# A decode layer on one core: wq as one transfer, finer last loads, and one copy moved to ScalarE

## The chip, the cores and the metric

The kernel runs on one core of one Trainium2 chip. The metric is device time in microseconds. "Median" is over the fast runs of a kernel: on one core that means that none was over 1.5% above the fastest of its kernel. A span quoted from a profile is about 2 us shorter than the time of the same execution (293.0 of 294.94 us for the kernel before). Each measurement is set against runs of the kernel before from the same rounds on the same chip.

## The reference, cut to what matters

A pre-norm decode step for a batch of 2 tokens of width 640: attention with 32 heads of 192 over the last 2048 positions of a cache, then a gated FFN of width 1536. Everything is bf16.

```python
x = A_x                                             # 2 x 1 x 640
h = x + attention(layernorm(x), k_cache, v_cache, wq, wo)
h2 = h + (gelu(ln @ w_gate) * (ln @ w_up)) @ w_down # ln = layernorm(h)
# wq: 640 x 6144    wo: 6144 x 640    w_gate, w_up: 640 x 1536    w_down: 1536 x 640
# K and V used: 2 x 32 x 2048 x 192 each, i.e. 50.3 MB each
```

The core has to read 122.29 MB for two tokens of output. There is little arithmetic per byte, so loads are the natural limit.

## The kernel before

All loads go through one DMA queue, issued in order by SyncE (called SP in the profile), into a ring of six slots of 24 KB per partition. K and V come in 16 groups of 3 MB each. A load may be issued when everything it overwrites has been used. Its issue order is K 0, wq, K 1, V 0, K 2, V 1, K 3, V 2, ..., then wo's last parts, w_gate, w_up and w_down.

```python
WQC = ((0, 2), (2, 4), (4, 5))
WDC = ((0, 3), (3, 6), (6, 9), (9, 12))
...
K_AT = (0, SLOT, 2 * SLOT, 3 * SLOT)
V_AT = (4 * SLOT, 5 * SLOT)
WQ_AT = (2 * SLOT, 3 * SLOT, 5 * SLOT)
WO_AT = (3 * SLOT, 3 * SLOT, 2 * SLOT, 0)
WD_AT = (2 * SLOT + 15360, 2 * SLOT + 19200, 15360, 19200)
...
        def load_wq():
            wq = A_wq.rearrange("(p c) n -> p c n", c=NC5)
            for i, (c0, c1) in enumerate(WQC):
                load(("wq", i), WQ_AT[i], 2 * (c1 - c0) * HQ * DH, wq[:, c0:c1, :],
                     lambda v: v.rearrange("p (c n) -> p c n", n=HQ * DH), f"wq{i}")
...
        def load_ffn():
            for key, at, w in (("wg", K_AT[1], B_w_gate), ("wu", K_AT[3], B_w_up)):
                load(key, at, 2 * NC5 * F, w.rearrange("(p c) f -> p c f", c=NC5),
                     lambda v: v.rearrange("p (c f) -> p c f", c=NC5), key)
            wd = B_w_down.rearrange("(r p j) n -> r p j n", p=128, j=3)
            for i, (f0, f1) in enumerate(WDC):
                load(("wd", i), WD_AT[i], 2 * (f1 - f0) * D, wd[i],
                     lambda v: v.rearrange("p (s n) -> p s n", n=D), f"wd{i}")
```

The queries are 80 matmuls over wq's five chunks; each part is used as it lands:

```python
        def q_rows():
            for i, (c0, c1) in enumerate(WQC):
                wq, wtoks = where["wq", i]

                def fn(e, c0=c0, c1=c1, wq=wq):
                    for c in range(c0, c1):
                        for J in range(4):
                            for r in range(4):
                                ins = e.matmul(tps[0][32 * r:32 * (r + 1), 0:384], lhsT=xnT[:, c, 32 * J:32 * (J + 1)],
                                               rhs=wq[:, c - c0, 1536 * J + 384 * r:1536 * J + 384 * (r + 1)],
                                               start=(c == 0 and J == 0), stop=(c == NC5 - 1 and J == 3), tile_position=(0, 32 * r))
                    return ins

                pe(fn, R=["xnT"] + wtoks, X=[("t", 0)])
                done(("wq", i))
```

At the end, when the loads run out, the FFN is a chain of small steps: normalised h (`hnT`), 20 matmuls with w_gate, a copy, transposes, gelu; then 20 matmuls with w_up, a copy, transposes, the product `uT`; then 48 matmuls with w_down in the blocks of `WDC`, a copy to `yrow`, and the store.

```python
        def ffn_columns(bank, xt, i):
            dve(lambda e: e.tensor_copy(grow[0:98, :], bank[0:98, 0:384]), W=["grow"], X=[xt])

            def fn(e):
                for j in range(3):
                    ins = e.transpose(tps[i][:, 128 * j:128 * j + 98], grow[0:98, j:384:3], identf[0:98, 0:98])
                return ins

            pe(fn, R=["grow", "identf"], X=[("t", i)])
            return tps[i][:, 0:384].rearrange("p (j r y) -> p r j y", j=3, y=32)[:, :, :, 0:2]
...
        ffn_in(sps, "s", "wg")
        gT = ffn_columns(sps, "s", 0)
        pe(h_rows, R=["hrow", ("hsel", 0), ("hsel", 1)], X=["m1"])
        ...                                         # gelu on VectorE and ScalarE
        ffn_in(ops_, "o", "wu")
        vT = ffn_columns(ops_, "o", 1)
        dve(tt(uT[...], vT, rjb(ga[:, 0, :]), ALU.mult), R=["ga0"], W=["uT"], X=[("t", 1)])
        for i, (f0, f1) in enumerate(WDC):
            ...                                     # 4 matmuls for each of the rows f0..f1 of w_down
        dve(lambda e: e.tensor_copy(yrow[0:98, :], m1[0:98, 0:160]), W=["y"], X=["m1"])
```

## Time and profile before

| | before |
|---|---|
| time, median of 3 runs | 294.95 us (294.79 to 294.95) |
| profiled span | 293.0 us |
| read from memory | 122.29 MB |
| busy: PE, DVE, ACT | 68%, 44%, 33% |
| the loading queue's share of 16 DMA engines | 97.8% |

Five lines of the page of the kernel before. The first two cut the span into 40 slices of 7.3 us: the busy share of the 16 DMA engines in tenths, and what they moved. The third is the loading queue (packets, MB, share of 16 engines' span), the fourth the chain of waits followed back from the end, the fifth the costliest group: its line, engine and operands, then busy us and mean ns of one, then idle us before it and what ended the idling.

```profile
DMA  7999999999999999999999999999999999999993
GB/s 279 436 427 433 431 440 435 430 425 430 425 420 438 430 433 427 430 430 430 430 421 436 430 430 430 430 430 433 430 430 430 430 430 430 430 430 426 430 406 125
q1 hardware_dynamic: 6632, 122.29, 97.8%
DMA 72%; PE 23%; SPq 2%; DVE 2%; issue 1%; ACT 0%
L549 PE MATMUL tps<-identf,ring 128*128 128x128 f32 x768 | 116.5, 320 | 46.4 <-DMA ring<-in_A_k_cache_dram 45.5
```

The DMA engines are full from the second slice to the last but one, near 430 GB/s. The Trainium skill, "DMA: Bandwidth & Descriptors", section "Where 436 GB/s comes from", gives 435.2 GB/s as the ceiling; this trace agrees with that to about 1%. PE mostly waits for K. So, leaving aside an earlier start of the loads, which the change doesn't touch, two things can make this kernel shorter: fewer DMA nanoseconds, or less work after the last byte has landed.

The timeline of the kernel before, at the end (start us, duration us, engine, line, instruction, and in brackets the idle time before it and who ended it; DMA landings show as releasers). PEld is PE's weight load.

```profile
284.26 0.71 PE L797 MATMUL m<-hrow,hsel 98*2 98x160 f32 x8
284.93 0.10 PEld L778 LDWEIGHTS ops<-ring,hnT 128*2 128x2 bf16 x8 [0.56 <-DMA ring<-in_B_w_up_dram]
284.93 1.77 PE L778 MATMUL ops<-ring,hnT 128*2 128x384 bf16 x20
286.75 0.56 DVE L785 COPY grow<-ops 98x384 f32<-98x384 f32 x1 [0.53 <-PE ops L778]
288.16 0.18 DVE L402 TENSOR_TENSOR uT<-tps,ga 128x24 bf16<-128x24 f32 x1 [0.86 <-PE tps L789]
288.40 1.84 PE L824 MATMUL m<-ring,uT 128*2 128x160 bf16 x48 [0.28 <-DVE uT L402]
289.67 0.23 PEld L824 LDWEIGHTS m<-ring,uT 128*2 128x2 bf16 x12 [0.24 <-DMA ring<-in_B_w_down_dram]
290.29 0.32 DVE L830 CAST yrow<-m 98x160 bf16<-98x160 f32 x1 [1.94 <-PE m L824]
```

The last 12 of the 48 w_down matmuls wait for the last landing (289.62 us in the trace's landing records, which hold the completion of each load by each of the 16 DMA engines; a load has landed when the last of the 16 is in).

The start, on SyncE's own row of the timeline: after K 0, wq, K 1 and V 0 have been issued, SyncE waits until wq's parts have been used.

```profile
1.45 1.63 SPq L342 DMA_DIRECT2D ring<-in_A_wq_dram  x3
...
20.49 0.54 SPq L342 DMA_DIRECT2D ring<-in_A_k_cache_dram  x1
31.98 0.54 SPq L342 DMA_DIRECT2D ring<-in_A_v_cache_dram  x1
32.56 0.61 SPq L342 DMA_DIRECT2D ring<-in_A_k_cache_dram  x1
```

These are K 2, V 1 and K 3.

### The profile page before, as it was taken

What the parts mean: (1) busy time and instruction counts of PE and PEld (TensorE: products, weight loads), DVE (VectorE), ACT (ScalarE), POOL (GpSimd) and SP (SyncE); (2) the same over time, 40 slices, a digit from 0 to 9 for tenths busy, and PEclk for the clock granted to TensorE, in tenths of its full rate; (3) what the DMA queues carried; (4) which work ended last, traced back from release to release, by engine and by line L of the source; (5) the groups of instructions that cost most, each with busy time, mean ns of one, the idle gap of its engine ahead of it and who ended that gap; (6) DMA issues with size and microseconds to landing.
All of it is one profiled execution on the core that took longest, in us unless ns stands there. A gap on an engine that the chain in (4) does not pass through costs nothing.

```text
span 293.0 us, 5065 instructions
## 1 busy us (share of the span) xinstructions
PE 198.8 (68%) x2141; PEld 153.0 (52%) x2141; DVE 128.5 (44%) x311; ACT 95.7 (33%) x119; POOL 8.4 (3%) x35
## 2 busy tenths in 40 slices
PE   2573586858677298849493597659696869666764
PEld 1451264838474285628281575356666666533432
DVE  5950364433447045525264155415365435532332
ACT  2150144433442143616161144234343434520000
POOL 3000100000000000000000000000000000000000
PEclk9996569795979579998899599969797968997755
DMA  7999999999999999999999999999999999999993
GB/s 279 436 427 433 431 440 435 430 425 430 425 420 438 430 433 427 430 430 430 430 421 436 430 430 430 430 430 433 430 430 430 430 430 430 430 430 426 430 406 125
DMA packets 6654, 122.44 MB, mean 418 GB/s; under 512 B 754, under 2 KB 756, under 8 KB 1396
## 3 DMA queue, kind: packets, MB, share of 16 engines
q1 hardware_dynamic: 6632, 122.29, 97.8%
q8 instruction: 7, 0.11, 0.2%
q14 instruction: 3, 0.02, 0.0%
q10 hardware_dynamic: 12, 0.00, 0.0%
HBM read 122.29 MB, written 0.00 MB: 417 GB/s over the span
## 4 chain that ended last, share of the span: by engine, by line
DMA 72%; PE 23%; SPq 2%; DVE 2%; issue 1%; ACT 0%
DMA ring<-in_A_k_cache_dram 54%; PE tps L549 16%; DMA ring<-in_A_wq_dram 10%; DMA ring<-in_A_wo_dram 9%; SPq L342 2%; PE ops L652 1%; PE m L703 1%; PE m L824 1%; PE sps L778 1%; PE ops L778 1%; PE m L685 1%; PE tps L789 1%; PE tps L571 1%; PE m L722 0%; DVE grow L785 0%
## 5 line engine op out<-in xcount | busy, mean ns | idle before, releaser
L549 PE MATMUL tps<-identf,ring 128*128 128x128 f32 x768 | 116.5, 320 | 46.4 <-DMA ring<-in_A_k_cache_dram 45.5
L549 PEld LDWEIGHTS tps<-identf,ring 128*128 128x128 f32 x768 | 107.3, 168 | 49.8 <-DMA ring<-in_A_k_cache_dram 46.9
L558 ACT ACTIVATE ktr<-tps 128x1024 bf16<-128x1024 bf16 x80 | 79.4, 1023 | 87.4 <-PE tps L549 87.4
L561 DVE COPY ktr<-tps 128x1024 bf16<-128x1024 bf16 x112 | 74.0, 687 | 74.5 <-PE tps L549 73.8
L627 ACT ACTIVATE eexp<-sm,nm 128x512 bf16<-128x512 f32 x16 | 11.5, 721 | 64.5 <-DVE nm L625 64.5
L652 PE MATMUL ops<-ring,ering 128*32 128x384 bf16 x512 | 24.4, 334 | 4.7 <-DMA ring<-in_A_v_cache_dram 4.7
L608 PE MATMUL sps<-ktr,rq 128*16 128x512 bf16 x384 | 25.9, 404 | 1.1 <-POOL rq L402 1.1
L616 DVE CUSTOM_DVE_ANT_1 sm<-sps,mska 128x512 f32<-128x512 f32 x16 | 11.1, 691 | 34.9 <-PE sps L608 34.9
L652 PEld LDWEIGHTS ops<-ring,ering 128*32 128x32 bf16 x512 | 12.5, 97 | 13.0 <-DMA ring<-in_A_v_cache_dram 6.0
L608 PEld LDWEIGHTS sps<-ktr,rq 128*16 128x16 bf16 x384 | 9.4, 90 | 12.1 <-issue 2.1
L623 PEld LDWEIGHTS m<-mrhs,pm 128*128 128x128 bf16 x16 | 1.5, 96 | 22.8 <-DVE mrhs L398 22.8
L623 PE MATMUL m<-mrhs,pm 128*128 128x16 bf16 x16 | 2.9, 184 | 14.7 <-DVE mrhs L398 14.7
L402 POOL TENSOR_TENSOR rq<-qs,mask 128x96 bf16<-128x96 bf16 x16 | 5.6, 359 | 195.9 <-PE sps L608 164.9
L571 PE MATMUL tps<-ring,xnT 128*32 128x384 bf16 x80 | 5.7, 444 | 7.4 <-DMA ring<-in_A_wq_dram 7.3
L402 DVE TENSOR_TENSOR ering<-m,mask 128x256 bf16<-128x256 f32 x16 | 6.7, 418 | 3.6 <-PE m L636 3.6
L571 PEld LDWEIGHTS tps<-ring,xnT 128*32 128x32 bf16 x80 | 2.4, 120 | 10.3 <-DMA ring<-in_A_wq_dram 8.3
L454 ACT ACTIVATE lt<-m,eps_t 128x2 f32<-128x2 f32 x2 | 0.5, 262 | 20.1 <-PE m L452 20.1
L594 DVE CAST qs<-ops 128x384 bf16<-128x384 f32 x1 | 0.6, 558 | 14.4 <-PE ops L589 14.4
L636 PE MATMUL m<-sel,eexp 128*128 128x64 bf16 x64 | 5.3, 213 | 1.2 <-ACT eexp L627 1.2
L636 PEld LDWEIGHTS m<-sel,eexp 128*128 128x128 bf16 x64 | 4.9, 114 | 1.7 <-DVE nm L625 1.3
L703 PE MATMUL m<-ring,ot 128*2 128x320 bf16 x96 | 4.9, 338 | 1.1 <-DMA ring<-in_A_wo_dram 1.1
L402 DVE TENSOR_TENSOR orow<-m,wm 128x1536 bf16<-128x1536 f32 x3 | 5.3, 1750 | 0.0
(113 smaller groups left out, 84.2 us busy)
## 6 DMA issues: line engine op xcount, KB each, us to landing
ring<-in_A_k_cache_dram SPq DMA_DIRECT2D x16, 3072.0 KB, 32.7
ring<-in_A_v_cache_dram SPq DMA_DIRECT2D x16, 3072.0 KB, 27.6
ring<-in_A_wq_dram SPq DMA_DIRECT2D x2, 3072.0 KB, 21.0
ring<-in_A_wo_dram SPq DMA_DIRECT2D x3, 1920.0 KB, 19.4
ring<-in_B_w_gate_dram SPq DMA_DIRECT2D x1, 1920.0 KB, 30.9
ring<-in_B_w_up_dram SPq DMA_DIRECT2D x1, 1920.0 KB, 27.0
ring<-in_B_w_down_dram SPq DMA_DIRECT2D x4, 480.0 KB, 28.9
ring<-in_A_wq_dram SPq DMA_DIRECT2D x1, 1536.0 KB, 27.9
```

What stands on the lines that cost most here:

```text
L342: P.op("sp", lambda e, v=v, src=src: e.dma_start(v, src), W=toks + [("sem", sem)], dma=sem)
L402: return lambda e: e.tensor_tensor(out=out, in0=a, in1=b, op=op)
L549: ins = e.transpose(tps[bi][:, 128 * u:128 * (u + 1)], kv[:, off:off + 128], identf[:, :])
L558: act(lambda e, dst=dst, bv=bv: e.activation(out=dst, in_=bv, func=ACT.Copy), W=[("kt", n)], X=[("t", bi)])
L561: dve(lambda e, dst=dst, bv=bv: e.tensor_copy(dst, bv), W=[("kt", n)], X=[("t", bi)], cls=0)
L571: ins = e.matmul(tps[0][32 * r:32 * (r + 1), 0:384], lhsT=xnT[:, c, 32 * J:32 * (J + 1)], rhs=wq[:, c - c0, 1536 * J + 384 * r:1536 * J + ...
L608: ins = e.matmul(sps[32 * ch:32 * ch + 16, :], lhsT=rq[:, g % 4, k, :], rhs=ktr[:, k // 2, 1024 * ch + k % 2:1024 * (ch + 1):2], start=(k ...
L616: dve(lambda e: e.tensor_tensor_reduce(out=sm[:, :].rearrange("p (u x) -> p u x", u=4), in0=sps[:, :].rearrange("p (u x) -> p u x", u=4), ...
L627: act(lambda e: e.activation(out=eexp[:, :], in_=sm[:, :], func=ACT.Exp, bias=nm[:, 0:1], scale=1.0, accum_out=zr[:, g % 4:g % 4 + 1]), R= ...
L636: ins = e.matmul(o, lhsT=eexp[:, 128 * u:128 * (u + 1)], rhs=sel64[:, :], start=True, stop=True)
L652: ins = e.matmul(ops_[32 * r:32 * (r + 1), 0:384], lhsT=ering[:, g % 4, t, :], rhs=vv[:, 384 * t:384 * (t + 1)], start=(g % 4 == 0 and t < 4),
L703: ins = e.matmul(m1[32 * r:32 * r + 2, 192:512], lhsT=ot[:, kk, :], rhs=wo[:, kk - k0, 320 * h:320 * (h + 1)], start=(kk == 1 or J < 2 and ...
```

## The change

Its intent, read from the diff: fewer and longer rows for wq (60 KB per partition, contiguous in memory) by laying it over two and a half slots; less PE work behind each of the last landings, by loading w_up as 4 + 1 chunks and w_down's last block as 2 + 1 rows; and the copy of up out of PSUM on ScalarE, which is idle there. The diff, with the second half of the mechanical edits cut:

```diff
-WQC = ((0, 2), (2, 4), (4, 5))
-WDC = ((0, 3), (3, 6), (6, 9), (9, 12))
+WDC = ((0, 3), (3, 6), (6, 9), (9, 11), (11, 12))
+WUC = ((0, 4), (4, 5))
 BIG = 1.0e9
-K_AT = (0, SLOT, 2 * SLOT, 3 * SLOT)
-V_AT = (4 * SLOT, 5 * SLOT)
-WQ_AT = (2 * SLOT, 3 * SLOT, 5 * SLOT)
-WO_AT = (3 * SLOT, 3 * SLOT, 2 * SLOT, 0)
-WD_AT = (2 * SLOT + 15360, 2 * SLOT + 19200, 15360, 19200)
+K_AT = (0, SLOT, 3 * SLOT, 5 * SLOT)
+V_AT = (2 * SLOT, 4 * SLOT)
+WQ_AT = 3 * SLOT + SLOT // 2
+WO_AT = (K_AT[3], K_AT[3], K_AT[2], 0)
+WD_AT = (K_AT[2] + 15360, K_AT[2] + 19200, 15360, 19200, 19200 + 2560)
 ...
-            for i, (c0, c1) in enumerate(WQC):
-                load(("wq", i), WQ_AT[i], 2 * (c1 - c0) * HQ * DH, wq[:, c0:c1, :],
-                     lambda v: v.rearrange("p (c n) -> p c n", n=HQ * DH), f"wq{i}")
+            load("wq", WQ_AT, 2 * NC5 * HQ * DH, A_wq.rearrange("(p c) n -> p c n", c=NC5),
+                 lambda v: v.rearrange("p (c n) -> p c n", n=HQ * DH), "wq")
 ...   # load_ffn: w_up in the chunks of WUC, w_down by the rows of WDC
 ...   # q_rows: one function with all 80 matmuls, behind the whole of wq
-        ffn_in(ops_, "o", "wu")
-        vT = ffn_columns(ops_, "o", 1)
+        ffn_in(ops_, "o", "wu", WUC)              # one PE step per chunk of WUC
+        act(lambda e: e.activation(out=urow[0:98, :], in_=ops_[0:98, 0:384], func=ACT.Copy), W=["urow"], X=["o"])
+        vT = ffn_columns(urow, "urow", tps[1], 1)
```

More of the change, by code (lines that the diff above doesn't have):

```diff
@@ L310, in bass_sequential_preLN__sliding_block_cached__geglu_ffn__decode_kernel @@
         grow = sb("grow", [128, 384], F32)
+        urow = sb("urow", [128, 384], F32)
         gsb = sb("gsb", [128, NF * B], F32)
@@ L358, in load_wq @@
         def load_wq():
-            wq = A_wq.rearrange("(p c) n -> p c n", c=NC5)
-            for i, (c0, c1) in enumerate(WQC):
-                load(("wq", i), WQ_AT[i], 2 * (c1 - c0) * HQ * DH, wq[:, c0:c1, :],
-                     lambda v: v.rearrange("p (c n) -> p c n", n=HQ * DH), f"wq{i}")
+            load("wq", WQ_AT, 2 * NC5 * HQ * DH, A_wq.rearrange("(p c) n -> p c n", c=NC5),
+                 lambda v: v.rearrange("p (c n) -> p c n", n=HQ * DH), "wq")
         def load_wo(J):
@@ L373, in load_ffn @@
         def load_ffn():
-            for key, at, w in (("wg", K_AT[1], B_w_gate), ("wu", K_AT[3], B_w_up)):
-                load(key, at, 2 * NC5 * F, w.rearrange("(p c) f -> p c f", c=NC5),
-                     lambda v: v.rearrange("p (c f) -> p c f", c=NC5), key)
+            load(("wg", 0), K_AT[1], 2 * NC5 * F, B_w_gate.rearrange("(p c) f -> p c f", c=NC5),
+                 lambda v: v.rearrange("p (c f) -> p c f", f=F), "wg")
+            for i, (c0, c1) in enumerate(WUC):
+                load(("wu", i), K_AT[3] + 2 * c0 * F, 2 * (c1 - c0) * F, B_w_up.rearrange("(p c) f -> p c f", c=NC5)[:, c0:c1, :],
+                     lambda v: v.rearrange("p (c f) -> p c f", f=F), f"wu{i}")
             wd = B_w_down.rearrange("(r p j) n -> r p j n", p=128, j=3)
             for i, (f0, f1) in enumerate(WDC):
-                load(("wd", i), WD_AT[i], 2 * (f1 - f0) * D, wd[i],
+                r = f0 // 3
+                load(("wd", i), WD_AT[i], 2 * (f1 - f0) * D, wd[r][:, f0 - 3 * r:f1 - 3 * r, :],
                      lambda v: v.rearrange("p (s n) -> p s n", n=D), f"wd{i}")
@@ L563, in q_rows, with fn @@
         def q_rows():
-            for i, (c0, c1) in enumerate(WQC):
-                wq, wtoks = where["wq", i]
-                def fn(e, c0=c0, c1=c1, wq=wq):
-                    for c in range(c0, c1):
-                        for J in range(4):
-                            for r in range(4):
-                                ins = e.matmul(tps[0][32 * r:32 * (r + 1), 0:384], lhsT=xnT[:, c, 32 * J:32 * (J + 1)],
-                                               rhs=wq[:, c - c0, 1536 * J + 384 * r:1536 * J + 384 * (r + 1)],
-                                               start=(c == 0 and J == 0), stop=(c == NC5 - 1 and J == 3), tile_position=(0, 32 * r))
-                    return ins
-                pe(fn, R=["xnT"] + wtoks, X=[("t", 0)])
-                done(("wq", i))
+            wq, wtoks = where["wq"]
+            def fn(e):
+                for c in range(NC5):
+                    for J in range(4):
+                        for r in range(4):
+                            ins = e.matmul(tps[0][32 * r:32 * (r + 1), 0:384], lhsT=xnT[:, c, 32 * J:32 * (J + 1)],
+                                           rhs=wq[:, c, 1536 * J + 384 * r:1536 * J + 384 * (r + 1)],
+                                           start=(c == 0 and J == 0), stop=(c == NC5 - 1 and J == 3), tile_position=(0, 32 * r))
+                return ins
+            pe(fn, R=["xnT"] + wtoks, X=[("t", 0)])
+            done("wq")
             act(lambda e: e.activation(
@@ L770, in bass_sequential_preLN__sliding_block_cached__geglu_ffn__decode_kernel, with ffn_in, fn, ffn_columns @@
                   lambda e: e.matmul(m2[:, 16:18], lhsT=rs[0:98, :].to_broadcast([98, 128]), rhs=bsel[0:98, :], start=True, stop=True))
-        def ffn_in(bank, xt, key):
-            wv, wtoks = where[key]
-            def fn(e):
-                for c in range(NC5):
-                    for r in range(4):
-                        ins = e.matmul(bank[32 * r:32 * r + 2, 0:384], lhsT=hnT[:, c, :], rhs=wv[:, c, 384 * r:384 * (r + 1)],
-                                       start=(c == 0), stop=(c == NC5 - 1), tile_position=(0, 32 * r))
-                return ins
-            pe(fn, R=["hnT"] + wtoks, X=[xt])
-        def ffn_columns(bank, xt, i):
-            dve(lambda e: e.tensor_copy(grow[0:98, :], bank[0:98, 0:384]), W=["grow"], X=[xt])
+        def ffn_in(bank, xt, key, parts):
+            for i, (c0, c1) in enumerate(parts):
+                wv, wtoks = where[key, i]
+                def fn(e, c0=c0, c1=c1, wv=wv):
+                    for c in range(c0, c1):
+                        for r in range(4):
+                            ins = e.matmul(bank[32 * r:32 * r + 2, 0:384], lhsT=hnT[:, c, :], rhs=wv[:, c - c0, 384 * r:384 * (r + 1)],
+                                           start=(c == 0), stop=(c == NC5 - 1), tile_position=(0, 32 * r))
+                    return ins
+                pe(fn, R=["hnT"] + wtoks, X=[xt])
+        def ffn_columns(row, tok, bank, i):
             def fn(e):
                 for j in range(3):
-                    ins = e.transpose(tps[i][:, 128 * j:128 * j + 98], grow[0:98, j:384:3], identf[0:98, 0:98])
+                    ins = e.transpose(bank[:, 128 * j:128 * j + 98], row[0:98, j:384:3], identf[0:98, 0:98])
                 return ins
-            pe(fn, R=["grow", "identf"], X=[("t", i)])
-            return tps[i][:, 0:384].rearrange("p (j r y) -> p r j y", j=3, y=32)[:, :, :, 0:2]
+            pe(fn, R=[tok, "identf"], X=[("t", i)])
+            return bank[:, 0:384].rearrange("p (j r y) -> p r j y", j=3, y=32)[:, :, :, 0:2]
         def h_rows(e):
@@ L802, in rjb @@
             return t.rearrange("p (r j b) -> p r j b", r=4, j=3)
-        ffn_in(sps, "s", "wg")
-        gT = ffn_columns(sps, "s", 0)
+        ffn_in(sps, "s", "wg", ((0, NC5),))
+        dve(lambda e: e.tensor_copy(grow[0:98, :], sps[0:98, 0:384]), W=["grow"], X=["s"])
+        gT = ffn_columns(grow, "grow", tps[0], 0)
         pe(h_rows, R=["hrow", ("hsel", 0), ("hsel", 1)], X=["m1"])
```

## The prediction

> **What bounds it.** Transfers. The page's slice table shows the 16 DMA engines at 90% or more in all slices but the first and last, moving about 430 GB/s; the queue table gives the loading queue 97.8% of 16 engines' span, for 122.29 MB. The Trainium skill, "DMA: Bandwidth & Descriptors", section "Where 436 GB/s comes from", puts the ceiling at 435.2 GB/s; the trace lies 1% under it. The chain of waits is 72% DMA. PE is busy 68%, DVE 44%, ACT 33%; the groups table gives PE 45.5 us idle before K transposes, released by K loads.
>
> **DMA cost of the change.** Bytes stay the same. The packet records show one row per packet: 3840 B in 149 ns, 15360 B in 575, 24576 B in 915: 7 ns + bytes at 27.1 GB/s. Each engine carries 8 rows of a transfer and a 9 ns semaphore write.
> - wq, one transfer instead of three: 16 rows and 2 semaphore writes fewer per engine, -0.13 us. A 61440 B row should take 2.28 us (estimate from the fit).
> - w_up and w_down: as many more, +0.13 us.
> Sum about zero; no rate gain from 60 KB rows.
>
> **wq stage.** Before, q's matmuls run on three landings (18.8, 26.7, 30.4 us) and end at 31.96. After, all 80 run behind the landing near 30.4; the last 64 took 4.2 us at a low granted clock, so 80 take 6 to 8 us and q comes about 5 us later (estimate). K 2, V 1 and K 3 can be issued only then, near 37 us instead of 20.5 and 32. K 1 and V 0 are queued from the start and keep the engines busy until 45.0 us: 7 us of margin. PE, idle 2 to 3 us before most K loads, recovers within about three groups. Effect on the end: none.
>
> **Tail.** By the timeline PE is busy with w_gate's work and h_rows until 284.97; w_up lands at 284.88. So loading w_up as 4 + 1 gains almost nothing. The ScalarE copy of 98x384 should take 0.50 us (estimate from ACT's 768 elements in 0.81 and 1024 in 1.02 us) against DVE's 0.56: uT 0.06 us sooner. The last w_down block lands at 289.62, PE's last 12 matmuls run 289.67 to 290.24, then yrow and the store. With 4 matmuls left, not 12, starting about 21 ns apart, the end comes about 0.15 us sooner: the only gain on the critical path.
>
> **Sum.** 294.95 - 0.2 = 294.75 us. Range 294.0 to 295.6. Chances: faster by over 2% 0.01, within 2% 0.97, slower by over 2% 0.02.
>
> **What would show it.** Right: wq rows near 2.28 us; the 430 GB/s plateau unbroken between 30 and 60 us; the K 1 transposes several us later, those of K 4 unmoved; the last w_down landing within 0.3 us of 289.6; its matmuls under 0.45 us; w_up's matmuls still begin near 285.0. Wrong: a dip of DMA share near 45 us; 60 KB rows off the fit; uT the last to arrive before the last w_down matmuls.
>
> **What could make it wrong.** The landing records show that the engines don't end together: of the last block's 16 shares nine land from 287.50 to 288.09, seven from 289.11 to 289.62. Lone rows of 1.1 to 1.5 us beside 16 KB instruction fetches show who was delayed, about 1.5 us each by the landings. The end is that of the unluckiest engine. If the change makes one engine be hit twice, about +1.5 us; if the slowest is spared, about -0.3 us. Beyond that, only 60 KB rows being handled unlike smaller ones would break it.

## The result, and the profile after

| | before | after |
|---|---|---|
| time, median of 5 runs | 294.95 us (294.79 to 295.00) | 294.62 us (294.40 to 294.69) |
| ratio of fast runs, 95% interval | | 0.9989 [0.9975, 1.0004] |
| profiled span | 293.0 us | 292.5 us |

A ratio is the mean time of one kernel's fast runs over that of the other's of the same rounds, so it is not quite the ratio of the medians. The interval just includes 1, but no run of the changed kernel reached the fastest run of the kernel before, and this happened again in a second set of five (run g_after below). The difference of the means is -0.32 us; the prediction was -0.2.

The page of the changed kernel, the lines that answer to those of before:

```profile
DMA  7998999999999999999999999999999999999993
GB/s 283 450 497 351 429 437 432 430 432 430 429 415 441 430 430 428 430 430 430 430 412 446 430 430 434 430 430 430 430 430 430 430 430 430 430 430 409 429 404 151
q1 hardware_dynamic: 6632, 122.29, 98.0%
DMA 75%; PE 20%; SPq 3%; DVE 1%; issue 0%
L551 PE MATMUL tps<-identf,ring 128*128 128x128 f32 x768 | 112.7, 314 | 46.6 <-DMA ring<-in_A_k_cache_dram 45.3
```

Nothing moved in the large. Slices 2 to 4 swing, at 450, 497 and 351 GB/s, but their average is 433; that long rows are counted in the slice where they start would explain it, and was not tested. The end of its timeline:

```profile
283.76 0.71 PE L797 MATMUL m<-hrow,hsel 98*2 98x160 f32 x8
283.99 0.41 PEld L780 LDWEIGHTS ops<-ring,hnT 128*2 128x2 bf16 x8
284.25 1.82 PE L780 MATMUL ops<-ring,hnT 128*2 128x384 bf16 x20
286.12 0.49 ACT L817 ACTIVATE urow<-ops 98x384 f32<-98x384 f32 x1 [1.16 <-PE ops L780]
287.46 0.18 DVE L404 TENSOR_TENSOR uT<-tps,ga 128x24 bf16<-128x24 f32 x1 [1.73 <-PE tps L789]
287.70 2.17 PE L826 MATMUL m<-ring,uT 128*2 128x160 bf16 x48 [0.28 <-DVE uT L404]
289.56 0.09 PEld L826 LDWEIGHTS m<-ring,uT 128*2 128x2 bf16 x4 [0.30 <-DMA ring<-in_B_w_down_dram]
289.92 0.32 DVE L832 CAST yrow<-m 98x160 bf16<-98x160 f32 x1 [2.28 <-PE m L826]
```

The last landing is at 289.52 (before 289.62), so the loads end nearly at the same time. What is shorter is the stretch behind it: from the last landing to the end of the w_down matmuls 0.34 us instead of 0.62. But w_up's matmuls begin 0.49 us behind the first of the eight h_rows matmuls, at 284.25, and uT is 0.70 us earlier than before. I had predicted that w_up's matmuls would still begin near 285.0. Not all of the 0.70 us is the change's doing: h_rows itself begins 0.50 us earlier, 0.24 of it because wo's last load landed earlier in this profile (275.50 for 275.74), 0.26 because wo's last 8 matmuls took 0.44 us at a granted clock (the share of PE's full speed that the profile records as allowed) of 1.00, against 0.70 us at 0.50 in the profile of the kernel before. This clock differs from profile to profile: two profiles of the changed kernel's tail, g_after and i_q2 below, show 0.48 and 0.70 us.

The start, on SyncE's row:

```profile
1.45 0.57 SPq L343 DMA_DIRECT2D ring<-in_A_wq_dram  x1
...
35.43 0.54 SPq L343 DMA_DIRECT2D ring<-in_A_k_cache_dram  x1
36.00 0.60 SPq L343 DMA_DIRECT2D ring<-in_A_v_cache_dram  x1
36.65 0.60 SPq L343 DMA_DIRECT2D ring<-in_A_k_cache_dram  x1
```

K 2 is now issued 15 us later than before, as foreseen, and the slices between 30 and 60 us show no dip.

The DMA packet records of the trace, one row per packet (median ns; these come from the trace's records, not from a view):

```
row bytes          3840   15360   12288   24576   61440   3072   2560   1280
before              149     575     460     915
after               152     575     465     915    2267    122    102     55
```

With 8 rows per engine and transfer and a 9 ns semaphore write at its end, the parts of the change cost, per engine: wq 2267 instead of 2 x 912 (the median of its own rows) + 460, -0.14 us and two semaphore writes less, -0.15 together; w_up 465 + 122 instead of 575, +0.10 us; w_down's last block 102 + 55 instead of 149, +0.07 us. That is +0.02 us, about zero as predicted.

### The profile page after: what moved, and what is told of

Same layout as the page of the kernel before. It is cut to its first block, busy times and chain, and to the rows that moved or that the text cites. A ratio compares the mean times of both kernels' runs of the same rounds, so it can differ in the third digit from the quotient of the medians.

```text
span 292.5 us, 5066 instructions
## 1 busy us (share of the span) xinstructions
PE 192.4 (66%) x2141; PEld 149.2 (51%) x2141; DVE 128.0 (44%) x310; ACT 96.0 (33%) x120; POOL 8.4 (3%) x35
## 4 chain that ended last, share of the span: by engine, by line
DMA 75%; PE 20%; SPq 3%; DVE 1%; issue 0%
DMA ring<-in_A_k_cache_dram 57%; PE tps L551 15%; DMA ring<-in_A_wq_dram 10%; DMA ring<-in_B_w_down_dram 8%; SPq L343 3%; PE tps L572 2%; PE ops L653 1%; PE m L704 1%; PE m L686 1%; DVE ktr L563 0%; DVE ering L404 0%; PE m L826 0%; PE m L637 0%; PE m L667 0%; DVE yrow L832 0%
## 5 line engine op out<-in xcount | busy, mean ns | idle before, releaser
L551 PE MATMUL tps<-identf,ring 128*128 128x128 f32 x768 | 112.7, 314 | 46.6 <-DMA ring<-in_A_k_cache_dram 45.3
L551 PEld LDWEIGHTS tps<-identf,ring 128*128 128x128 f32 x768 | 104.1, 164 | 50.2 <-DMA ring<-in_A_k_cache_dram 46.6
L609 PE MATMUL sps<-ktr,rq 128*16 128x512 bf16 x384 | 24.6, 389 | 1.1 <-POOL rq L404 1.1
L572 PEld LDWEIGHTS tps<-ring,xnT 128*32 128x32 bf16 x80 | 3.1, 132 | 13.3 <-issue 11.2
L579 ACT ACTIVATE qrow<-tps 128x768 bf16<-128x768 f32 x1 | 0.8, 810 | 15.6 <-PE tps L572 15.6
L637 PE MATMUL m<-sel,eexp 128*128 128x64 bf16 x64 | 4.6, 196 | 1.2 <-ACT eexp L628 1.2
L704 PE MATMUL m<-ring,ot 128*2 128x320 bf16 x96 | 4.1, 298 | 1.6 <-DMA ring<-in_A_wo_dram 1.6
```

Of the source, the lines that this page charges most:

```text
L551: ins = e.transpose(tps[bi][:, 128 * u:128 * (u + 1)], kv[:, off:off + 128], identf[:, :])
L609: ins = e.matmul(sps[32 * ch:32 * ch + 16, :], lhsT=rq[:, g % 4, k, :], rhs=ktr[:, k // 2, 1024 * ch + k % 2:1024 * (ch + 1):2], start=(k ...
L637: ins = e.matmul(o, lhsT=eexp[:, 128 * u:128 * (u + 1)], rhs=sel64[:, :], start=True, stop=True)
L704: ins = e.matmul(m1[32 * r:32 * r + 2, 192:512], lhsT=ot[:, kk, :], rhs=wo[:, kk - k0, 320 * h:320 * (h + 1)], start=(kk == 1 or J < 2 and ...
```

## The experiments

Twelve kernels, each timed against the kernel before in the same rounds. "Difference" is between the means of the fast runs; its standard error, worked out from the scatter of the runs, is 0.04 to 0.09 us. "Tail" is from the last landing to the end of the last w_down matmul, in the profiled run. "Ledger" is the change of the tail (0.615 us before) plus the row costs above, and it uses nothing from the timed runs.

| run | what is changed from before | difference us | tail us | ledger us |
|---|---|---|---|---|
| a_wd | w_down 2 + 1 | +0.01 | 0.510 | -0.03 |
| b_wq | wq in one transfer | -0.08 | 0.614 | -0.15 |
| c_wu | w_up 4 + 1 | +0.14 | 0.613 | +0.10 |
| d_act | copy on ScalarE | -0.01 | 0.614 | 0.00 |
| e_wd_wu | w_down and w_up | -0.14 | 0.347 | -0.09 |
| f_nowq | all but wq | -0.14 | 0.347 | -0.09 |
| g_after | the whole change again | -0.31 | 0.345 | -0.25 |
| l_nowu | all but w_up | -0.32 | 0.437 | -0.26 |
| i_q2 | the change, q's matmuls twice | -0.22 | 0.346 | |
| i_q4 | the change, q's matmuls four times | +3.53 | 0.346 | |
| h_wq4 | the change, 4/5 of wq loaded | -4.04 | 0.347 | |
| k_fetch | the change, 1024 idle GpSimd instructions | +2.87 | 0.344 | |

No 95% interval of the nine small ones (the first eight and i_q2) is clear of 1, so no single time settles anything; the argument rests on the traces, one profile for each run, and the times agree with them within their errors.

The landing records give a check on the row costs that needs no end time: the mean landing of the last load's 16 shares, one for each DMA engine. It is 288.38 us before and 288.42 in d_act, which loads the same; 288.48 in a_wd, 288.50 in c_wu and 288.58 in e_wd_wu, where rows were added; 288.31 in b_wq, where rows were saved; and 288.53 in f_nowq against 288.44 in the changed kernel and in g_after.

### Each part alone

Theory T was that w_down's split alone carries the gain. Rival R was the wq transfer, rival R2 the earlier uT.

**a_wd**

```diff
-WDC = ((0, 3), (3, 6), (6, 9), (9, 12))
-WD_AT = (2 * SLOT + 15360, 2 * SLOT + 19200, 15360, 19200)
+WDC = ((0, 3), (3, 6), (6, 9), (9, 11), (11, 12))
+WD_AT = (2 * SLOT + 15360, 2 * SLOT + 19200, 15360, 19200, 19200 + 2560)
 ...   # load_ffn: w_down by these rows
```

> Only w_down's last block in 2 + 1 rows. Theory T (the gain is the shorter work behind the last landing): before, PE needed 0.57 us from the first of the last 12 matmuls to the end of the last, in the changed kernel 0.30 us for 4; so this part alone gives -0.2 to -0.3 us, and carries the whole gain of the change. Rival R (the gain comes from the wq transfer, through fewer transfers or another pattern of delayed DMA engines): 0.0 +- 0.1 us here.

Measured 294.89 us against 294.78 (ratio 1.0001, 0.9988 to 1.0015). T fell. The timeline of a_wd shows why:

```profile
284.82 0.10 PEld L779 LDWEIGHTS ops<-ring,hnT 128*2 128x2 bf16 x8 [0.83 <-DMA ring<-in_B_w_up_dram]
...
288.29 1.77 PE L825 MATMUL m<-ring,uT 128*2 128x160 bf16 x48 [0.28 <-DVE uT L403]
290.11 0.33 DVE L831 CAST yrow<-m 98x160 bf16<-98x160 f32 x1 [1.88 <-PE m L825]
```

All 48 w_down matmuls run in one unbroken 1.77 us behind uT; there is no wait for the last block any more (it landed at 289.55), and yet they end at 290.06. PE had started them too late to be done sooner.

**b_wq**: the wq lines and the slot layout of the change alone, with w_down's old four blocks.

```diff
-WQC = ((0, 2), (2, 4), (4, 5))
-WQ_AT = (2 * SLOT, 3 * SLOT, 5 * SLOT)
+WQ_AT = 3 * SLOT + SLOT // 2
 ...   # the other offsets, load_wq and q_rows as in the change
```

> Only wq in one transfer of 60 KB rows with the new slots. T: 0.0 +- 0.1 us; the landing of wq comes near 29.6 us instead of 30.4 as in the changed kernel, K 2 is issued near 35.4 us, and the last w_down landing stays within 0.3 us of 289.6. R: -0.3 us, and the last w_down landing is earlier by as much.

294.76 us against 294.78 (0.9998, 0.9984 to 1.0011), K 2 issued late as in the changed kernel (34.6 us), tail unchanged. R fell as the whole cause: it asked for -0.3 us, and the difference is -0.08 with a standard error of 0.07. Part of it stands, for the rows save 0.15 us by the records. The last landing of this profile, 289.33, is 0.30 us earlier than before, as R had said; but d_act, where no load was changed, landed at 289.43, so one last landing decides nothing.

**c_wu**

```diff
+WUC = ((0, 4), (4, 5))
 ...   # load_ffn and ffn_in by these chunks
-        ffn_in(ops_, "o", "wu")
+        ffn_in(ops_, "o", "wu", WUC)
```

> Only w_up in 4 + 1 rows. T: 0.0 to +0.1 us (8 rows and one semaphore write more per engine, about 0.07 us of DMA); w_up's matmuls still start near 285.0, behind h_rows. A second rival, R2 (uT came 0.7 us earlier in the changed kernel, and that is the gain): -0.2 us here or with the ScalarE copy.

294.94 us against 294.78 (1.0004, 0.9991 to 1.0018): no gain, as T said, but not for T's reason. w_up's matmuls did start earlier, at 284.45 and 0.49 us behind h_rows, and uT with them. The gain was then lost in the wait for the last block:

```profile
284.45 1.82 PE L782 MATMUL ops<-ring,hnT 128*2 128x384 bf16 x20
...
287.97 1.37 PE L828 MATMUL m<-ring,uT 128*2 128x160 bf16 x36 [0.28 <-DVE uT L405]
289.72 0.57 PE L828 MATMUL m<-ring,uT 128*2 128x160 bf16 x12 [0.39 <-DMA ring<-in_B_w_down_dram]
```

**d_act**

```diff
-            dve(lambda e: e.tensor_copy(grow[0:98, :], bank[0:98, 0:384]), W=["grow"], X=[xt])
+            row, tok = (grow, "grow") if i == 0 else (urow, "urow")
+            if i == 0:
+                dve(lambda e: e.tensor_copy(row[0:98, :], bank[0:98, 0:384]), W=[tok], X=[xt])
+            else:
+                act(lambda e: e.activation(out=row[0:98, :], in_=bank[0:98, 0:384], func=ACT.Copy), W=[tok], X=[xt])
 ...   # the transposes read row
```

(`i` is 1 for up; gate's copy stays on VectorE.)

> Only the up copy on ScalarE. T: the copy takes 0.49 us for 0.56, uT comes 0.06 us sooner, the time does not move (0.0 +- 0.1 us), because the last 12 w_down matmuls wait for their landing at 289.6 all the same. R2: -0.1 to -0.2 us.

294.77 us against 294.78 (1.0001, 0.9987 to 1.0015). The copy took 0.49 us, uT came sooner, and the last 12 matmuls waited all the same. R2 fell too.

### The parts together

So the new theory M: the end is the later of two paths. L is the last landing plus the matmuls behind it, 0.62 us with 12 of them and 0.345 with 4. P is the start of the w_down matmuls plus 1.77 us for 48 in a row. In the kernel before, L is 290.24 and P 290.17, only 0.07 us apart: to shorten one uncovers the other. Where w_up comes in one load, P hangs on its landing: in before, a_wd, b_wq, d_act and l_nowu w_up's matmuls start 0.04 us behind it, whenever h_rows was. Where it is split, they start 0.49 us behind the first h_rows matmul in every profile, and P hangs on PE's earlier work instead.

**e_wd_wu**: the edits of a_wd and c_wu together.

> w_down's and w_up's splits together, nothing else. New theory M: the end is the later of two paths, L = last landing + 0.34 us (4 matmuls; 0.62 with 12) and P = start of the w_down matmuls (uT) + 1.77 us for 48 in a row. Before: L 290.24, P 290.17. w_down's split alone leaves P (290.06 in its run), w_up's alone leaves L (290.29). M: together uT comes 0.4 us sooner and L is short, so -0.2 to -0.3 us, w_down matmuls ending within 0.36 us of the last landing. Rival W: the three parts that were tried alone (0.0 each) add to 0.0 here, and the gain of the change needs the wq transfer: 0.0 +- 0.1 us.

294.76 us against 294.92 (0.9995, 0.9981 to 1.0009). The tail is 0.347 us, inside M's 0.36, where neither part alone brought it under 0.51. In time it is -0.14 us, short of M's -0.2 to -0.3. M had left out what the two splits cost in rows, 0.17 us; with that the ledger says -0.09. W's 0.0 +- 0.1 us is not excluded by the time or by the ledger; what the tail excludes is W's reason, that the splits together do nothing. Its timeline:

```profile
284.28 0.71 PE L802 MATMUL m<-hrow,hsel 98*2 98x160 f32 x8
...
284.77 1.82 PE L783 MATMUL ops<-ring,hnT 128*2 128x384 bf16 x20
...
288.29 1.81 PE L829 MATMUL m<-ring,uT 128*2 128x160 bf16 x48 [0.28 <-DVE uT L406]
289.79 0.09 PEld L829 LDWEIGHTS m<-ring,uT 128*2 128x2 bf16 x4 [0.22 <-DMA ring<-in_B_w_down_dram]
```

The last 4 matmuls wait for the last landing (289.75), so L binds, but only just: P is 290.05 and L 290.10, because wo's last 8 matmuls took 0.70 us here at a clock of 0.50. In f_nowq and the changed kernel, where they took 0.44, P lies 0.35 and 0.40 us ahead of L.

**f_nowq**: the edits of a_wd, c_wu and d_act together.

> All of the change but wq's one transfer. M: as the pair of splits, -0.2 to -0.3 us, since L ends it already; uT 0.07 us sooner again, without effect. W: 0.0 +- 0.1 us.

294.82 us against 294.92 (0.9997, 0.9983 to 1.0011), mean -0.14 us, again short of M's -0.2 to -0.3 for the same reason, tail 0.347: ScalarE's copy adds nothing once L ends the kernel, as M says.

**g_after**: the changed kernel unaltered.

> The changed kernel once more, on the same chip and rounds. M: -0.25 to -0.45 us, i.e. the pair of splits plus at most 0.15 us from 16 rows and 2 semaphore writes less in wq. W: -0.3 us, clear of the kernel without wq's part.

294.62 us against 294.92 (0.9989, 0.9975 to 1.0002), mean -0.31 us. Against f_nowq the wq transfer is worth 0.17 us here, and 0.08 us alone in b_wq, against 0.15 us from the row records. Both have standard errors of 0.07 to 0.08 us, so the records' figure is the better one. The mean landings above agree in sign, with 0.09 us for wq in both comparisons (b_wq against the mean of before and d_act, the changed kernel against f_nowq). So wq pays back a good part of the 0.17 us that the finer splits cost; whether it pays back all of it is not settled.

**l_nowu**: the changed kernel with one load of w_up.

```diff
-WUC = ((0, 4), (4, 5))
+WUC = ((0, 5),)
```

> The changed kernel with w_up in one load again. M: uT comes about 0.4 us later relative to the loads, so path P (uT + 1.77 us) binds again: the w_down matmuls end 0.42 to 0.47 us after the last landing instead of 0.345; the saved rows give back about 0.07 us; sum 0.0 to +0.1 us against the changed kernel, so -0.2 to -0.3 us against the kernel before. If w_up's split had been worthless, as I predicted, this would be 0.07 us faster than the changed kernel, with 0.345 us after the last landing.

294.46 us against 294.82 (0.9989, 0.9976 to 1.0003), mean -0.32 us. Its timeline:

```profile
284.71 0.10 PEld L780 LDWEIGHTS ops<-ring,hnT 128*2 128x2 bf16 x8 [0.55 <-DMA ring<-in_B_w_up_dram]
...
288.11 1.77 PE L826 MATMUL m<-ring,uT 128*2 128x160 bf16 x48 [0.28 <-DVE uT L404]
289.94 0.32 DVE L832 CAST yrow<-m 98x160 bf16<-98x160 f32 x1 [1.88 <-PE m L826]
```

The wait for w_up is back, the 48 matmuls again run unbroken in 1.77 us, and the tail is 0.437 us, inside M's 0.42 to 0.47: P binds. What that loses in the tail (0.09 us) is what the saved rows give back (0.10 us). So the split of w_up does shorten a path, and in the whole kernel no net gain or loss of it is seen (l_nowu's -0.32 us against g_after's -0.31, with standard errors of 0.09 and 0.04). No run is clear of the changed kernel, and none points to a version that beats both.

### What bounds the rest

**h_wq4** (wrong result on purpose; PE's work is the same):

```diff
-load("wq", WQ_AT, 2 * NC5 * HQ * DH, A_wq.rearrange("(p c) n -> p c n", c=NC5), ...
+load("wq", WQ_AT, 2 * (NC5 - 1) * HQ * DH, A_wq.rearrange("(p c) n -> p c n", c=NC5)[:, 0:NC5 - 1, :], ...
-rhs=wq[:, c, ...
+rhs=wq[:, min(c, NC5 - 2), ...
```

> The changed kernel with 4 of the 5 chunks of wq loaded (48 KB rows; the fifth chunk's product reads the fourth, so the result is wrong on purpose; PE's work is the same). If bytes bound the time: 1.573 MB less at 430 GB/s is -3.66 us against the changed kernel, 290.9 to 291.1 us. If something on the engines bound it, less than half of that.

290.89 us. Less g_after's 294.62 from the same rounds that is -3.73 us, for 1.57 MB less, as its page says:

```profile
q1 hardware_dynamic: 6632, 120.72, 97.9%
```

Bytes bound the time: 3.73 us for the 3.66 expected. That q also ended earlier here doesn't explain it, for the next run moves q's end without effect.

**i_q2** (and **i_q4** with 4): PE's work on q doubled.

```diff
+                for _ in range(2):
                     for c in range(NC5):
                         for J in range(4):
 ...   # the body as before, indented
```

> The changed kernel with q's 80 matmuls done twice (same result; PE's work for q doubled). In the changed kernel K 2 was issued at 35.4 us and the queue's work lasted until 44.8 us. Doubling adds 4 to 6 us, so K 2 is issued at 39 to 41 us. Theory (the late q is paid from a margin): nothing reaches the end, 294.6 +- 0.15 us. Rival (every us of q's delay shows at least in part, because PE has to catch up): +1 us or more.

294.60 us, with K 2 issued at 38.16, a little before the 39 to 41 us expected:

```profile
38.16 0.54 SPq L343 DMA_DIRECT2D ring<-in_A_k_cache_dram  x1
```

That is 0.09 us over g_after's difference, with standard errors of 0.05 and 0.04 us: a delay of 2.7 us costs nothing that can be seen.

> The same, q's matmuls done four times: 11 to 17 us later, K 2 issued at 46 to 52 us, after the queue has run dry near 44 us. Theory: the margin is overdrawn, DMA share shows a gap between 44 and 50 us, and the end moves by the length of the gap, the issue time of K 2 less 44 us and about 1.4 us until its first packet: +3.5 to +9.5 us, to be computed from the measured issue. Rival: no gap or a much smaller loss.

298.38 us, with K 2 issued at 44.79, earlier than I had thought because PE ran most of the 320 matmuls at the full granted clock (0.50 until 32 us, 1.00 from 33 us on). One-microsecond windows of i_q4 (length, busy us of each engine with the number of instructions, granted clock, DMA share, GB/s):

```profile
41.00:42.00 1.00, 1.00 (x32) 0.70 (x28) 0.00 (x0) 0.00 (x0) 0.00 (x0) 1.00 0.92 385
42.00:43.00 1.00, 1.00 (x29) 0.58 (x22) 0.00 (x0) 0.00 (x0) 0.00 (x0) 1.00 0.56 221
43.00:44.00 1.00, 0.77 (x21) 0.43 (x19) 0.00 (x0) 0.00 (x0) 0.00 (x0) 1.00 0.12 49
44.00:45.00 1.00, 0.76 (x19) 0.28 (x11) 0.00 (x0) 0.20 (x1) 0.00 (x0) 1.00 0.06 16
45.00:46.00 1.00, 0.34 (x12) 0.34 (x12) 0.00 (x0) 0.61 (x1) 0.00 (x0) 1.00 0.00 0
46.00:47.00 1.00, 0.19 (x7) 0.07 (x3) 0.77 (x4) 0.00 (x0) 0.13 (x1) 1.00 1.21 393
```

The gap is there. By the packet records 13 of the 16 engines ran dry between 42.6 and 43.2 us and the last at 44.6; K 2's first packets start at 46.13, 1.34 us behind the issue. The gap is thus 3.0 to 3.5 us before the first packet for these engines, and the end moved by 3.53 us against before and 3.8 us against the changed kernel (i_q4's and g_after's differences). My formula had used 44 us for the dry queue and gives 2.2 us: it was too small, because I had read the dry queue from V 0's last landing, which is the slowest engine's (44.94 us here, where the first share landed at 43.02). The lesson is in the margin of the changed kernel: for no engine to run dry, K 2 has to be issued by about 41.3 us (an estimate, 42.6 less 1.34) and is issued at 35.4, so 5.9 us of margin were left, of which i_q2 used 2.7 without a trace.

**k_fetch**

```diff
+        junk = sb("junk", [128, 1024], mybir.dt.uint8)
...
+        for k in range(1024):
+            pool(lambda e, k=k: e.memset(junk[:, k:k + 1], 0))
```

> The changed kernel with 1024 one-byte-wide memsets on GpSimd (idle then) after its last rq, near 200 us; they do nothing but have to be fetched. If 16 KB instruction fetches delay the DMA engine they use by 1.5 us each and the slowest engine sets the end: about four more fetches appear after 200 us, the landing records show more than seven late shares or some two hits late, and the end moves by 0 (only engines spared so far are hit), +1.5 us (one is hit twice) or more. Rival (fetches are noise): the spread of the last landing stays as it is, seven late and nine early, and the time stays within 0.15 us.

297.77 us, +2.87 us against before and about 3.2 us over the changed kernel, for instructions that compute nothing needed, on an engine with nothing else to do. The memsets on GpSimd's timeline:

```profile
209.75 4.28 POOL L763 MEMSET junk<- 128x1 uint8 x128 [0.35 <-issue]
214.96 4.28 POOL L763 MEMSET junk<- 128x1 uint8 x128 [0.93 <-issue]
```

Every 128 of them there is a pause, and the packet records show one 8 KB packet on an instruction queue, eight in all, with the row beside each taking 1265 ns instead of 915. The landing records of the last transfer show who paid (us, one share for each of the 16 DMA engines):

```
before   287.50 287.51 287.56 287.59 287.67 287.73 287.73 287.85 288.09   289.11 289.15 289.19 289.21 289.21 289.32 289.62
after    287.45 287.51 287.55 287.64 287.74 287.78 287.85 287.88 288.38   288.91 289.16 289.25 289.45 289.45 289.50 289.52
k_fetch  287.41 287.43 287.45 287.45 287.80 287.88 287.89 288.08   288.89 289.23 289.28 289.29 289.30 289.31 289.54 292.68
```

One share of k_fetch is 3.1 us behind the next: all eight fetches fell on one engine. The packet records name no engine, but each packet starts within 5 ns of the end of the one before it on the same engine, which sorts them into 16 sequences (where two fitted, the closer was taken), and all eight fetches lie in one. They cost it 309 ns for the packet and 350 ns in the data row behind it each time, 5.3 us in sum, which is its distance from the first of the early group. The expectation was wrong in form (eight small fetches on one engine, not four large ones on several) and right in the point: the end is that of the unluckiest engine, and the rival, noise, fell.

## Why the prediction was right, and where it was not

- **The bound.** Right: DMA bytes. h_wq4 took 3.73 us off for 1.57 MB.
- **DMA cost of the change, zero.** Right: rows of 60 KB took 2267 ns (estimate 2280), and the records add up to +0.02 us: -0.15 for wq and +0.17 for the splits, where I had 0.13 for both.
- **The wq stage, free.** Right. q ended at 35.4 us, 3.4 us later and not 5: the 80 matmuls took 5.6 us, under my 6 to 8 (the trace of before has 48 matmuls in the 4.2 us that I had ascribed to 64), and wq landed at 29.6 us, 0.8 us sooner than before. K 1's transposes began at 41.8 instead of 38.8, K 4's at 81.8 instead of 81.6. The margin was 5.9 us, not 7, because I took the last landing, the slowest engine's, for the moment at which the engines run dry.
- **"So loading w_up as 4 + 1 gains almost nothing."** The reason was wrong. I read the end of h_rows, 284.97, as the moment at which PE is free. The Trainium skill, "Perfetto Trace Analysis", section "Tensor Engine Instruction (MATMUL, LD_WEIGHTS)", says that the end that the profiler gives a TensorE instruction is estimated from its size. It is not the moment at which the next may start: in the changed kernel w_up's matmuls start at 284.25, h_rows is drawn until 284.47. The line of PE's weight loads, idle 0.56 us until w_up's landing, had said before the run that PE was waiting. How long is read by comparison: 0.67 us from h_rows' first matmul to w_up's first before, 0.49 where nothing is waited for, so 0.18 us in that profile. Measured against the last landing, the split starts the w_down matmuls 0.2 to 0.5 us sooner (e_wd_wu against a_wd, c_wu against before); which of the two depends on the clock that wo's last matmuls got (0.50 in e_wd_wu, 1.00 in c_wu).
- **"With 4 matmuls left, not 12 ... about 0.15 us sooner: the only gain on the critical path."** The number of the sum was about right, the step was not, and that is in part luck: I took the saving too small and did not see the path that could have taken a third of it back. Behind the landing the saving is 0.27 us, nearly twice my estimate; 0.07 us of new rows in the same transfer go against it; and w_down's split alone gets only 0.10 us of it (a_wd), since 48 matmuls need 1.77 us from uT on and uT was too late. I had treated the end as one path, and it was two, 0.07 us apart. With w_up's split beside it the full 0.27 us is there (e_wd_wu); with ScalarE's copy and the wq transfer instead, 0.18 us of it (l_nowu).
- **ScalarE's copy.** Right in size (0.49 us for 0.56). Its worth depends on which path binds: nothing alone (d_act), nothing beside the two splits (f_nowq). What l_nowu has over a_wd, 0.07 us of tail, is this copy: from w_up's landing to the first w_down matmul it takes 3.52 us in before, a_wd and b_wq, and 3.44 to 3.45 us in d_act and l_nowu, so wq has no part in it.
- **Instruction fetches.** The risk was real, and the change did not touch it: seven late shares before and after. k_fetch shows what it costs when it goes wrong.

Total: -0.2 predicted, -0.32 and -0.31 measured, -0.25 by the ledger. What the ledger lacks, about 0.06 us, is within the scatter of the last landing from run to run, 289.3 to 289.8 in the profiles of the kernels that load everything and are not delayed on purpose.

## What to carry to other kernels

When a kernel is bound by its loads, work out the end as several paths, each from its own last landing, and see how far apart they are before you shorten one: two changes that give nothing alone can give all of it together. Judge whether PE is free by when its next weight load starts and what released it, not by the drawn end of its last matmul. Count what a finer split costs in rows, and put the longest contiguous rows where a later use does no harm, as with wq here, which had 5.9 us to spare.

## What the Trainium skill lacked or had wrong

- "DMA: Bandwidth & Descriptors", section "Where 436 GB/s comes from", says in its warning that for transfers between HBM and SBUF the HBM side (about 358 GB/s) binds. Read by itself this does not fit this kernel: its one core held 430 GB/s for some 270 us and 418 GB/s over the whole span, close under the 435 GB/s ceiling. The condition is there, but not in the warning: the same page's section "Measured (HBM→SBUF, 128 partitions, SWDGE, issued from GpSimd)" says that about 358 GB/s is what each core gets when both cores of the HBM domain stream.
- "Runtime: NRT & Kernel Launch", section "Instruction fetch mechanics", calls the cost of crossing a block boundary "mostly hidden". For the engine that runs the instructions that may be so; the DMA engine that fetches is delayed by about 1.5 us by a 16 KB block (a packet of 1.0 us, then a row 0.5 us longer), and each 8 KB block of k_fetch also cost GpSimd a pause of 0.9 us.
- The same section gives blocks of 16 KiB or 256 instructions. GpSimd's memsets in k_fetch were fetched in blocks of 8 KB and paused every 128 instructions.
- I found no page that says how fetches spread over the 16 DMA engines. In k_fetch all eight from one instruction stream fell on one engine, and the kernel ended 3.1 us later than its second slowest engine.
- "DMA: Bandwidth & Descriptors" has no cost of a row above 4 KB on the SyncE queue. Here it was 7 ns + bytes at 27.1 GB/s per engine from 3.8 to 24.6 KB, and a 61440 B row took 2267 ns, 10 ns under that line.
